# Intermediate columns in batch order, and their loads queued behind the experts' weights, in an attention, MoE and FFN kernel

## The chip, the cores and the metric

The kernel runs on one core of a Trainium2 chip. The metric is device time in microseconds (us) of one execution; the value compared is the median of several runs.

## What is computed

Three stages follow each other; B = 4 batches of S = 576 tokens, 2304 tokens in all, 512 features.

```
x = attention(q, k, v, omega)         # random features, 8 heads, per batch
e = argmax(x @ w_gate)                # an expert for each token
y = gate * (relu(x @ w1[e]) @ w2[e])  # 512 -> 1024 -> 512
h = y @ w_in                          # 512 -> 2048
out = (h * sigmoid(1.702 h)) @ w_out  # 2048 -> 512
```

The inputs are such that the tokens of a batch go to one expert in the main; a loop behind the main part does tokens that go elsewhere.

## The kernel before

All matrix products of the second and third stage are made of three products of halves: an operand is split into a high part (rounded by ACT) and a low part (the rest, by DVE or POOL), and `mm3` (line 110) issues high x high, high x low and low x high into one bank of PSUM.

Attention and experts run interleaved, batch by batch; the code writes the work in an order, and a scheduler then fixes the order of instructions on every engine before the run. An engine takes its instructions strictly in that order, so the first one that has to wait holds up all behind it.

The expert of a batch (`moe_gen`, line 689) takes the 576 tokens in two halves of HS = 288. For each half, layer one makes 8 feature tiles with 4 x 3 matmuls each (tile m_ps), which ACT turns into h1h (relu, line 683) and DVE into h1l (line 686); layer two makes 4 output tiles with 8 x 3 matmuls each, one in a bank of tag m (m_ps) and three in banks of tag a (w_ps), in the last batch or so all four at a time, weights outermost. Half a batch is thus 192 matmuls of 288 columns. DVE takes an output tile out as y (line 736), ACT rounds it to yh (739), POOL, or DVE in the last batch, makes yl (741), and SP stores both to HBM (line 754).

The expert's weights come in eight pieces of 512 KB, c = 0 to 3 of w1 and 4 to 7 of w2 (`stage`, line 611; the DMA is line 623, tile st, two buffers). Each piece is split by ACT into wh (645) and by DVE or POOL into wl (647); a buffer is free for the piece after next once both are done.

y lies in HBM as five chunks of columns, CHUNKS = 512, 512, 512, 512, 256. Columns are ordered in pairs of batches: 512 tokens of the first batch, 512 of the second, then the 64 + 64 tokens that are left of both (`ycol`, line 657). A chunk is loaded by `load_y` (line 882) once all batches that it needs are counted as done: chunks 0 and 1 after batches 0 and 1, chunk 2 after batch 2, chunks 3 and 4 after batch 3. The third stage multiplies each tile f of 128 features of w_in by each chunk c (`first`, tile f_ps, 12 matmuls) in the order f < 3 with c < 3, then c = 3 and 4, then f = 3 and on. `prep_in` (line 851) loads two tiles of w_in (tile raw, line 841, 512 KB each), DVE decodes them (dec), ACT and DVE split them (wi). The result goes through the sigmoid form of gelu to HBM (g_dram) and comes back for blocks of 256 columns (`load_g`), each of which makes two tiles of 128 output rows (`out_rows`).

The transfers of SP stand in one queue. Loads of y, w_in and expert weights are written as jobs that the loop over the last batches calls once a step:

```
        jobs.queue += [load_y(ly, 0), load_y(ly, 1)]
        for n, c in enumerate(Mg):
            tick()
            if wp is None and x_done[0] >= B - 1:
                ...
                jobs.queue += [prep_in(wp, ly, 0), load_y(ly, 2), prep_in(wp, ly, 1)]
            jobs()
```

Of the kernel before, what the change touches and what calls it, by code (L numbers as in the profile page):

```python
# [22 lines left out]
def kernel(  # L23
# [13 lines left out]
    nc = tc.nc  # L37
# [12 lines left out]
    CHUNKS = (4 * P, 4 * P, 4 * P, 4 * P, 2 * P)  # L50
# [57 lines left out]
    wo_dram = dram.tile([7, P, NF2 // 2, DM // 2], F32, name="wo_dram")  # L108

# [547 lines left out]
    def ycol(b, c):  # L657
        base = (b // 2) * 2 * S
        return base + (b % 2) * T * P + c if c < T * P else base + 2 * T * P + (b % 2) * TAIL + c - T * P
# [8 lines left out]
    def moe_gen(b):  # L668
# [3 lines left out]
        for hf in range(2):  # L672
# [46 lines left out]
            for dt in range(KD):  # L719
# [23 lines left out]
                def store(yh=yh, yl=yl, dt=dt, hf=hf):  # L743
                    lo, hi = hf * HS, (hf + 1) * HS
                    for a, z in ((lo, min(hi, T * P)), (max(lo, T * P), hi)):
                        if a < z:
                            o = ycol(b, a)
                            cut = min(z, a + CH - o % CH)
                            for x, e in ((a, cut), (cut, z)):
                                if x == e:  # L750
                                    continue
                                ch, q0 = divmod(o + x - a, CH)
                                for i, t in enumerate((yh, yl)):
                                    nc.sync.dma_start(  # L754
                                        out=y_dram[ch][i][dt * P:(dt + 1) * P, q0:q0 + e - x],
                                        in_=f32(t[:, x - lo:e - lo]),
                                    )
# [3 lines left out]
                if not outer:  # L761
                    yield 1.46
                    pump(1)
        prep["free"] = 2 * NW * (b + 2)

        def count():
            done[0] += 1

        lag(4, count)
# [68 lines left out]
    def load_raw(pool, s, f):  # L838
        raw = pool.tile([P, DM], I64, tag="raw", name="raw", bufs=2)
        if s == 0:  # L840
            nc.sync.dma_start(
                out=raw.rearrange("p (k f) -> p k f", k=KD),
                in_=w_in[:, f * P:(f + 1) * P].rearrange("(k p) f -> p k f", p=P),
            )
        else:
            nc.sync.dma_start(out=raw, in_=w_out[f * P:(f + 1) * P, :])
        return raw
# [3 lines left out]
    def prep_in(pool, rpool, j):  # L851

        raws = [load_raw(rpool, 0, 2 * j + i) for i in range(2)]
# [28 lines left out]
    def load_y(pool, c):  # L882
        while done[0] < (1, 2, 3, 4, 4)[c]:
            yield 1
        y = pool.tile([P, 2, KD, CHUNKS[c]], F32R, tag=f"y{c}", name=f"y{c}", bufs=1)
        for i in range(2):
            nc.sync.dma_start(out=f32(y[:, i]), in_=y_dram[c][i].rearrange("(k p) n -> p k n", p=P))
            if c < 3 and not i:
                yield 3
        y_t[c] = (y[:, 0], y[:, 1])  # L890

    done = [0]
# [10 lines left out]
    if True:  # L903
# [47 lines left out]
        jobs.queue += [load_y(ly, 0), load_y(ly, 1)]  # L951
        for n, c in enumerate(Mg):
            tick()
            if wp is None and x_done[0] >= B - 1:
# [3 lines left out]
                jobs.queue += [prep_in(wp, ly, 0), load_y(ly, 2), prep_in(wp, ly, 1)]  # L958
            jobs()
# [3 lines left out]
        jobs.queue += [load_y(ly, 3), load_y(ly, 4)]  # L963
# [5 lines left out]
        def out_rows(ti):  # L969
            pr, j = divmod(ti, 9)  # L970
            b0 = 2 * pr
            if j < 8:
                b, t = b0 + j // T, j % T
                return [(0, P, out[b * S:b * S + T * P].rearrange("(p t) c -> p t c", t=T)[:, t, :])]
            return [(i * TAIL, TAIL, out[(b0 + i) * S + T * P:(b0 + i + 1) * S, :]) for i in range(2)]
# [42 lines left out]
        def load_g(k, gt, halves=(0, 1)):  # L1018

            c, o = divmod(2 * k * P, CH)  # L1020
            for h in halves:
                nc.sync.dma_start(
                    out=gt[:, h], in_=g_dram[c][h][:, :, o:o + 2 * P].rearrange("f p n -> p f n")
                )
# [276 lines left out]
```

## Time and profile before

| | |
|---|---|
| median of 3 runs | 793.82 us (791.28 to 793.97) |
| profiled execution, its own time | 793.09 us |
| span of the profile (first to last instruction) | 791.3 us |
| mean granted clock of TensorE | 0.987 |
| DMA, mean | 172 GB/s, 136.01 MB |

The stages in the trace: attention with the experts of batches 0 to 2 up to about 320 us, what is left of the experts up to about 411 us, y @ w_in to 605 us, then the product with w_out. In the views below PE is TensorE's matmuls, PEld its weight loads, DVE, ACT, POOL the other engines, SPq the queue of SP. A value in brackets with an arrow is the time an engine stood idle before an instruction and what ended it. The granted clock is a share of 2.4 GHz: 0.50 is 1.2 GHz.

### The profile page before, as it was taken

To read this page: it belongs to the slowest core of one execution; us is meant where nothing else is said; L and a number is where in the kernel's file an instruction comes from. 1 tells how busy PE (TensorE), PEld (TensorE's weight loads), DVE (VectorE), ACT (ScalarE), POOL (GpSimd) and SP (SyncE) were. 2 spreads that over 40 slices of the span, in tenths; PEclk is the share of its full clock that TensorE was granted. 3 is DMA by queue.
4 is the path that set the end of the run, shared out by engine and by line. 5 is a ranking of instruction groups with operands and counts; after the bars stand their busy time and mean duration, and the time that the engine had idled before them with its cause. 6 is when DMAs were issued, how large, how long until landed. Compare 5 with 4: busy or idle time off the path is not lost.

```text
span 791.3 us, 14276 instructions
## 1 busy us (share of the span) xinstructions
PE 762.6 (96%) x5538; PEld 710.2 (90%) x5538; DVE 452.6 (57%) x1026; ACT 305.0 (39%) x575; POOL 177.4 (22%) x134
## 2 busy tenths in 40 slices
PE   7998999999999999979999999999999999999996
PEld 6877899999999999979997888888889999999996
DVE  5877776577764353447320656525044777777761
ACT  5545563345433341423111332244334334434330
POOL 3565297458302450201000223210000000000000
PEclk9999899999999999989999999999999999999998
DMA  5456775368624330698517999993476443444401
GB/s 158 119 141 155 220 205 140 86 155 223 152 53 136 117 93 27 208 296 244 178 30 239 332 385 322 371 386 129 139 229 210 134 134 133 134 134 133 133 28 31
DMA packets 151418, 136.01 MB, mean 172 GB/s; under 512 B 63024, under 2 KB 129840, under 8 KB 150448
## 3 DMA queue, kind: packets, MB, share of 16 engines
q1 hardware_dynamic: 139824, 116.16, 48.3%
q10 hardware_dynamic: 11520, 18.88, 6.5%
q8 instruction: 45, 0.74, 0.4%
q14 instruction: 29, 0.24, 0.1%
HBM read 83.41 MB, written 45.11 MB: 162 GB/s over the span
## 4 chain that ended last, share of the span: by engine, by line
PE 76%; DMA 11%; DVE 4%; SPq 3%; issue 2%; POOL 2%; ACT 2%; POOLq 0%; DVEq 0%; ACTq 0%
PE f_ps L112 22%; PE m_ps L112 15%; PE qa L1049 13%; PE qm L1049 7%; PE pb L1049 3%; DMA st<-in_moe_w_dram 3%; PE w_ps L112 3%; PE num L416 3%; DMA raw<-in_moe_w_in_dram 3%; DMA m<-in_k_dram 2%; PE kv_ps L374 2%; SPq L754 2%; PE pr L316 2%; DMA m<-in_q_dram 2%; PE tq L402 1%
## 5 line engine op out<-in xcount | busy, mean ns | idle before, releaser
L112 PE MATMUL f_ps<-y,wi 128*128 128x512 f32 (+1 forms) x960 | 198.4, 368 | 1.7 <-DMA y<-y_dram 1.7
L112 PEld LDWEIGHTS f_ps<-y,wi 128*128 128x128 f32 x960 | 167.0, 189 | 32.0 <-DMA y<-y_dram 2.1
L1049 PE MATMUL qa<-wo,gs 128*128 128x256 f32 x864 | 107.2, 282 | 0.0
L1049 PEld LDWEIGHTS qa<-wo,gs 128*128 128x128 f32 x864 | 104.8, 190 | 0.0
L995 ACT ACTIVATE g<-f_ps 128x512 f32<-128x512 f32 (+1 forms) x80 | 43.7, 554 | 104.3 <-PE f_ps L112 65.5
L112 PE MATMUL m_ps<-xh,wh 128*128 128x288 f32 x256 | 79.0, 309 | 3.9 <-DVE y L736 3.1
L112 PE MATMUL m_ps<-xh,wl 128*128 128x288 f32 x256 | 76.8, 300 | 0.0
L112 PE MATMUL m_ps<-xl,wh 128*128 128x288 f32 x256 | 76.6, 299 | 0.0
L647 POOL TENSOR_TENSOR wl<-st,wh 128x1024 fp32r<-128x1024 f32 x23 | 54.6, 2382 | 44.9 <-ACT wh L645 41.3
L686 DVE SCALAR_TENSOR_TENSOR h1l<-m_ps,h1h 128x288 fp32r<-128x288 f32 x64 | 28.9, 454 | 62.1 <-ACT h1h L683 62.0
L814 ACT ACTIVATE gs<-s 128x1024 fp32r<-128x1024 f32 x27 | 28.6, 1061 | 75.0 <-DVE s L1034 59.8
L331 DVE TENSOR_REDUCE small<-pr 128x4 f32<-128x512 f32 (+1 forms) x80 | 51.1, 639 | 10.0 <-PE pr L323 5.0
L1049 PE MATMUL qm<-wo,gs 128*128 128x256 f32 x432 | 54.5, 282 | 0.0
L876 POOL TENSOR_TENSOR z<-z 128x256 f32<-128x256 f32 x32 | 25.4, 814 | 127.6 <-DMA g_dram<-g 76.1
L112 PEld LDWEIGHTS m_ps<-xh,wh 128*128 128x128 f32 x256 | 48.7, 190 | 5.3 <-DVE y L736 3.6
L1049 PEld LDWEIGHTS qm<-wo,gs 128*128 128x128 f32 x432 | 52.8, 190 | 0.1
L645 ACT ACTIVATE wh<-st 128x1024 fp32r<-128x1024 f32 (+1 forms) x33 | 34.0, 1032 | 43.5 <-DMA st<-in_moe_w_dram 26.9
L815 DVE TENSOR_TENSOR gs<-gt,gs 128x1024 fp32r<-128x1024 f32 x36 | 44.2, 1226 | 10.4 <-ACT gs L814 9.9
L112 PEld LDWEIGHTS m_ps<-xl,wh 128*128 128x128 f32 x256 | 48.7, 190 | 0.3
L112 PEld LDWEIGHTS m_ps<-xh,wl 128*128 128x128 f32 x256 | 48.8, 191 | 0.0
L112 PE MATMUL m_ps<-h1h,wh 128*128 128x288 f32 x160 | 48.8, 306 | 0.0
L112 PE MATMUL m_ps<-h1h,wl 128*128 128x288 f32 x160 | 47.8, 300 | 0.0
(156 smaller groups left out, 1444.8 us busy)
## 6 DMA issues: line engine op xcount, KB each, us to landing
gt<-g_dram SPq DMA_DIRECT2D x18, 1024.0 KB, 7.2
g_dram<-g ACTq DMA_DIRECT2D x64, 256.0 KB, 5.4
st<-in_moe_w_dram SPq DMA_DIRECT2D x31, 512.0 KB, 4.5
y<-y_dram SPq DMA_DIRECT2D x8, 1024.0 KB, 8.8
raw<-in_moe_w_in_dram SPq DMA_DIRECT2D x16, 512.0 KB, 6.4
raw<-in_moe_w_out_dram SPq DMA_DIRECT2D x16, 512.0 KB, 6.3
wo<-wo_dram SPq DMA_DIRECT2D x7, 1024.0 KB, 7.8
wo_dram<-z SPq DMA_DIRECT2D x8, 768.0 KB, 7.8
```

What stands on the lines that cost most here:

```text
L112: ins = nc.tensor.matmul(out=ps, lhsT=a, rhs=b, start=start and n == 0, stop=stop and n == 2)
L316: nc.tensor.matmul(out=ps[:, :, h2], lhsT=xT[:, (2 * pr + h2) * 2 + t0 // 2], rhs=wbd)
L331: nc.vector.tensor_reduce(out=pm, in_=ps[:, :w], axis=AX.X, op=ALU.max, negate=on_act)
L416: nc.tensor.matmul(out=ps[:n, c, h2, :], lhsT=lhsT, rhs=kv[:, h, :])
L645: nc.scalar.activation(out=hi[:, :, s], in_=st[:, :, s], func=ACTF.Copy)
L647: eng.tensor_tensor(out=lo[:, :, s], in0=st[:, :, s], in1=f32(hi)[:, :, s], op=ALU.subtract)
L686: nc.vector.scalar_tensor_tensor(out=hl[:, f], in0=ps, scalar=0.0, in1=f32(hh[:, f]), op0=ALU.max, op1=ALU.subtract)
L814: nc.scalar.activation(out=hi, in_=src, func=ACTF.Copy)
L815: nc.vector.tensor_tensor(out=lo, in0=src, in1=f32(hi), op=ALU.subtract)
L876: nc.gpsimd.tensor_tensor(out=z[:, o], in0=z[:, a], in1=z[:, b], op=op)
L995: nc.scalar.activation(out=g, in_=ps, func=ACTF.Gelu_apprx_sigmoid)
L1049: ins = nc.tensor.matmul(out=ps, lhsT=x[:, f], rhs=w[i][:, f], start=start and f + m == 0, stop=f == NP - 1 and m == 2, skip_group_check=True,
```

## The change

The columns of y are now in the plain order of batches, in chunks of 512, 512, 512, 480 and 288. `pieces` says in which chunks a run of columns lies. Batches are 576 columns, halves 288: chunks 0 to 3 are 2016 columns, seven halves exactly, and chunk 4 is the last half of batch 3. Work done is counted by halves, and `load_y` waits for the halves that a chunk needs, so chunk 3 does not wait for the last half. The loads of chunks 0 and 1 are no longer asked for as soon as the attention is over: all jobs start when the last expert piece has been staged (`prep["staged"] == 2 * NW * B`), and `behind` ties a load of y, or one of the first four tiles of w_in, to the four entries of SP's queue that were written ahead of it, so that the scheduler puts it after them; no wait is added on the chip. Output rows of a tile are stored in the pieces that the new order gives, two of 64 rows where a tile runs over a boundary, and the eighth block of g is read from chunks 3 and 4 (224 and 32 columns).

```diff
-    CHUNKS = (4 * P, 4 * P, 4 * P, 4 * P, 2 * P)
+    CHUNKS = (4 * P, 4 * P, 4 * P, 480, 288)
...
+    def behind(ins, n):
+
+        eng, me = ins.ins.engine, ins.ins.name
+        found = [i for i in reversed(nc.cur_bb.bb.instructions) if i.engine == eng and i.name != me][:n]
+        for x in found:
+            tc.add_manual_dep(
+                ins.ins, x.name,
+                mybir.DependencyInfo(mybir.DependencyClass.NoSync, mybir.DependencyReason.DATA),
+                reason="behind",
+            )
...
-    def ycol(b, c):
-        base = (b // 2) * 2 * S
-        return base + (b % 2) * T * P + c if c < T * P else base + 2 * T * P + (b % 2) * TAIL + c - T * P
+    done = [0]
+
+    def pieces(c, n):
+
+        found, x = [], 0
+        while x < n:
+            ch = next(i for i in range(NCH) if c + x < sum(CHUNKS[:i + 1]))
+            o = c + x - sum(CHUNKS[:ch])
+            m = min(n - x, CHUNKS[ch] - o)
+            found.append((x, m, ch, o))
+            x += m
+        return found
...
-                    lo, hi = hf * HS, (hf + 1) * HS
-                    for a, z in ((lo, min(hi, T * P)), (max(lo, T * P), hi)):
-                        if a < z:
-                            o = ycol(b, a)
-                            cut = min(z, a + CH - o % CH)
-                            for x, e in ((a, cut), (cut, z)):
-                                if x == e:
-                                    continue
-                                ch, q0 = divmod(o + x - a, CH)
-                                for i, t in enumerate((yh, yl)):
-                                    nc.sync.dma_start(
-                                        out=y_dram[ch][i][dt * P:(dt + 1) * P, q0:q0 + e - x],
-                                        in_=f32(t[:, x - lo:e - lo]),
-                                    )
+                    for x, n, ch, o in pieces(b * S + hf * HS, HS):
+                        for i, t in enumerate((yh, yl)):
+                            nc.sync.dma_start(
+                                out=y_dram[ch][i][dt * P:(dt + 1) * P, o:o + n], in_=f32(t[:, x:x + n])
+                            )
...
+            def count():
+                done[0] += 1
+
+            lag(4, count)
...
-    def load_raw(pool, s, f):
+    def load_raw(pool, s, f, after=0):
         raw = pool.tile([P, DM], I64, tag="raw", name="raw", bufs=2)
         if s == 0:
-            nc.sync.dma_start(
+            ins = nc.sync.dma_start(
                 out=raw.rearrange("p (k f) -> p k f", k=KD),
                 in_=w_in[:, f * P:(f + 1) * P].rearrange("(k p) f -> p k f", p=P),
             )
+            behind(ins, after)
...
-        raws = [load_raw(rpool, 0, 2 * j + i) for i in range(2)]
+        raws = [load_raw(rpool, 0, 2 * j + i, 4 if j < 2 else 0) for i in range(2)]
...
-        while done[0] < (1, 2, 3, 4, 4)[c]:
+        while done[0] * HS < sum(CHUNKS[:c + 1]):
             yield 1
         y = pool.tile([P, 2, KD, CHUNKS[c]], F32R, tag=f"y{c}", name=f"y{c}", bufs=1)
         for i in range(2):
-            nc.sync.dma_start(out=f32(y[:, i]), in_=y_dram[c][i].rearrange("(k p) n -> p k n", p=P))
-            if c < 3 and not i:
+            behind(nc.sync.dma_start(out=f32(y[:, i]), in_=y_dram[c][i].rearrange("(k p) n -> p k n", p=P)), 4)
+            if c + 1 < NCH and not i:
                 yield 3
         y_t[c] = (y[:, 0], y[:, 1])
...
-        jobs.queue += [load_y(ly, 0), load_y(ly, 1)]
         for n, c in enumerate(Mg):
             tick()
             if wp is None and x_done[0] >= B - 1:
                 flush()
                 xep.release()
                 wp = tc.alloc_tile_pool(name="wp", bufs=1)
-                jobs.queue += [prep_in(wp, ly, 0), load_y(ly, 2), prep_in(wp, ly, 1)]
-            jobs()
+                jobs.queue += [prep_in(wp, ly, 0), load_y(ly, 0), load_y(ly, 1), prep_in(wp, ly, 1)]
+                jobs.queue += [load_y(ly, 2), load_y(ly, 3)]
+            if prep["staged"] == 2 * NW * B:
+                jobs()
         flush()
         while jobs.busy():
             jobs()
-        jobs.queue += [load_y(ly, 3), load_y(ly, 4)]
+        jobs.queue.append(load_y(ly, 4))
...
-            pr, j = divmod(ti, 9)
-            b0 = 2 * pr
-            if j < 8:
-                b, t = b0 + j // T, j % T
-                return [(0, P, out[b * S:b * S + T * P].rearrange("(p t) c -> p t c", t=T)[:, t, :])]
-            return [(i * TAIL, TAIL, out[(b0 + i) * S + T * P:(b0 + i + 1) * S, :]) for i in range(2)]
+
+            found, c = [], ti * P
+            while c < (ti + 1) * P:
+                b, k = divmod(c, S)
+                p0 = c - ti * P
+                if k < T * P:
+                    t, p = divmod(k, P)
+                    n = min(P - p, (ti + 1) * P - c)
+                    dst = out[b * S:b * S + T * P].rearrange("(p t) c -> p t c", t=T)[p:p + n, t, :]
+                else:
+                    n = min(S - k, (ti + 1) * P - c)
+                    dst = out[b * S + k:b * S + k + n, :]
+                found.append((p0, n, dst))
+                c += n
+            return found
...
-            c, o = divmod(2 * k * P, CH)
             for h in halves:
-                nc.sync.dma_start(
-                    out=gt[:, h], in_=g_dram[c][h][:, :, o:o + 2 * P].rearrange("f p n -> p f n")
-                )
+                for x, n, c, o in pieces(2 * k * P, 2 * P):
+                    nc.sync.dma_start(
+                        out=gt[:, h, :, x:x + n], in_=g_dram[c][h][:, :, o:o + n].rearrange("f p n -> p f n")
+                    )
```

On SP, where the expert of batch 2 stores its first half and batch 3's weights are being staged (yh, yl are what is stored, st the staged weights, raw w_in), before:

```order
L754 DMA y20_dram_69<-yh_4389 128x288
L887 DMA y0_4015<-y00_dram_65 128x4x512
L887 DMA y0_4015<-y01_dram_66 128x4x512
L887 DMA y1_4205<-y10_dram_67 128x4x512
L887 DMA y1_4205<-y11_dram_68 128x4x512
L754 DMA y21_dram_70<-yl_4390 128x288
L623 ISA
L623 DMA st_4459<-in_moe_w1_dram 128x4x256
```

and now, the rows in the same place, then those around the loads, six stagings later:

```order
L766 DMA y21_dram_70<-yl_4384 128x288
L634 ISA
L634 DMA st_4453<-in_moe_w1_dram 128x4x256
L634 ISA
L634 DMA st_4489<-in_moe_w1_dram 128x4x256
```

and, behind the last staging:

```order
L634 DMA st_4638<-in_moe_w2_dram 128x2x512
L852 DMA raw_4652<-in_moe2_w_in_dram 128x4x128
L852 DMA raw_4654<-in_moe2_w_in_dram 128x4x128
L899 DMA y0_4656<-y00_dram_65 128x4x512
L899 DMA y1_4658<-y10_dram_67 128x4x512
L899 DMA y0_4656<-y01_dram_66 128x4x512
L899 DMA y1_4658<-y11_dram_68 128x4x512
```

The four loads of chunks 0 and 1 went from ahead of piece 2 of the weights to behind piece 7 (st_4638), with the first two tiles of w_in.

On ACT, in the same stage, layer one of batch 2's second half (h1h) and the splits of batch 3's weights (wh1 is piece 1, wh2 piece 2); before:

```order
L645 ACTIVATE wh1_4476<-st_4228 128x1024
L683 ACTIVATE h1h_4392<-m_ps_4461 128x288
L683 ACTIVATE h1h_4392<-m_ps_4480 128x288
L683 ACTIVATE h1h_4392<-m_ps_4497 128x288
L683 ACTIVATE h1h_4392<-m_ps_4516 128x288
L683 ACTIVATE h1h_4392<-m_ps_4533 128x288
L645 ACTIVATE wh2_4512<-st_4459 128x1024
```

and now:

```order
L656 ACTIVATE wh1_4470<-st_4223 128x1024
L703 ACTIVATE h1h_4386<-m_ps_4455 128x288
L703 ACTIVATE h1h_4386<-m_ps_4474 128x288
L656 ACTIVATE wh2_4506<-st_4453 128x1024
L703 ACTIVATE h1h_4386<-m_ps_4491 128x288
L703 ACTIVATE h1h_4386<-m_ps_4510 128x288
L656 ACTIVATE wh3_4542<-st_4489 128x1024
L703 ACTIVATE h1h_4386<-m_ps_4527 128x288
L656 ACTIVATE wh4_4592<-st_4525 128x1024
```

The splits of pieces 2 and 3, which stood behind the last relu of the half, now stand among them: piece 2 ahead of the last three, piece 3 ahead of the last one; piece 4 follows the last. On DVE the low halves of the same pieces moved in the same way, and those of pieces 4, 5 and 6 stand among the evictions y of batch 2 and ahead of the first h1l of batch 3.

On SP, the last stores of batch 3 and the loads behind them; before:

```order
L754 DMA y40_dram_73<-yh_5252 128x128
L754 DMA y41_dram_74<-yl_5253 128x128
L754 DMA y40_dram_73<-yh_5252 128x64
L754 DMA y41_dram_74<-yl_5253 128x64
L887 DMA y3_5287<-y30_dram_71 128x4x512
L887 DMA y3_5287<-y31_dram_72 128x4x512
L887 DMA y4_5290<-y40_dram_73 128x4x256
```

and now:

```order
L766 DMA y40_dram_73<-yh_5247 128x288
L766 DMA y41_dram_74<-yl_5248 128x288
L899 DMA y4_5266<-y40_dram_73 128x4x288
L899 DMA y4_5266<-y41_dram_74 128x4x288
L858 DMA raw_5290<-in_moe2_w_out_dram 128x512
```

The last half is eight stores instead of 24, and chunk 3 is loaded (y3_5071) ahead of them.

## Rows read from the trace of the kernel before

**Rows 1.** The page, part 1: engine, busy us (share of the span), instructions.
```profile
PE 762.6 (96%) x5538; PEld 710.2 (90%) x5538; DVE 452.6 (57%) x1026; ACT 305.0 (39%) x575; POOL 177.4 (22%) x134
```

**Rows 2.** Waits of PE from 320 to 435 us: who, us in total, times, longest.
```profile
PE m_ps L112 <- DVE y L736: 3.1, 2, 2.2
PE w_ps L112 <- ACT wh L645: 2.3, 1, 2.3
PE f_ps L112 <- DMA y<-y_dram: 1.7, 1, 1.7
```

**Rows 3.** Timeline of PE: start us, duration us, instruction, count, [idle before].
```profile
335.59 0.29 PE L112 MATMUL w_ps<-h1l,wh 128*128 128x288 f32 x1
...
345.01 0.30 PE L112 MATMUL m_ps<-xh,wh 128*128 128x288 f32 x1
...
348.90 0.40 PE L112 MATMUL m_ps<-xh,wh 128*128 128x288 f32 x1 [2.15 <-DVE y L736]
...
353.37 0.61 PE L112 MATMUL w_ps<-h1h,wh 128*128 128x288 f32 x1 [2.35 <-ACT wh L645]
...
410.84 19.70 PE L112 MATMUL f_ps<-y,wi 128*128 128x512 f32 x86
...
432.19 172.07 PE L112 MATMUL f_ps<-y,wi 128*128 128x512 f32 x845 [1.66 <-DMA y<-y_dram]
```

**Rows 4.** Chain that ended last, one piece: start us, us, what, count.
```profile
388.91 3.20 PE m_ps L112 x24
```

**Rows 5.** Timeline of PE, a gap in the attention.
```profile
186.93 1.12 PE L402 MATMUL tq<-ident,qp 128*128 128x128 f32 x4 [1.31 <-DVE xl L445]
```

**Rows 6.** Windows: busy us of PE, PEld, DVE, ACT, POOL; granted clock; DMA share; GB/s.
```profile
187.00:190.00 3.00, 3.00 (x20) 2.94 (x21) 2.83 (x8) 1.69 (x4) 3.00 (x2) 0.52 0.68 225
352.00:354.00 2.00, 0.61 (x1) 0.29 (x1) 2.00 (x4) 1.62 (x4) 0.98 (x1) 0.50 0.85 238
432.00:434.00 2.00, 1.80 (x8) 1.51 (x9) 0.00 (x0) 0.60 (x1) 0.00 (x0) 1.00 1.08 389
```

**Rows 7.** Timeline of SP's queue: start us, us, issue, count.
```profile
329.19 2.78 SPq L887 DMA_DIRECT2D y<-y_dram  x4
332.02 0.53 SPq L754 DMA_DIRECT2D y_dram<-yl  x1
332.81 2.30 SPq L623 DMA_DIRECT2D st<-in_moe_w_dram  x1
...
422.06 2.31 SPq L887 DMA_DIRECT2D y<-y_dram  x4
```

**Rows 8.** Tile st, from 300 to 375 us: issue to landing.
```profile
DMA to landing us min/median/max: 3.5/5.1/13.0
```

**Rows 9.** The page, part 6: issues, KB each, median us to landing.
```profile
st<-in_moe_w_dram SPq DMA_DIRECT2D x31, 512.0 KB, 4.5
y<-y_dram SPq DMA_DIRECT2D x8, 1024.0 KB, 8.8
```

**Rows 10.** Timeline of ACT.
```profile
333.26 0.41 ACT L683 ACTIVATE h1h<-m_ps 128x288 fp32r<-128x288 f32 x1 [2.38 <-PE m_ps L112]
...
345.83 1.06 ACT L645 ACTIVATE wh<-st 128x1024 fp32r<-128x1024 f32 x1 [6.85 <-DMA st<-in_moe_w_dram]
```

**Rows 11.** Timeline of DVE.
```profile
346.92 1.23 DVE L647 TENSOR_TENSOR wl<-st,wh 128x1024 fp32r<-128x1024 f32 x1 [7.46 <-ACT wh L645]
...
348.40 0.45 DVE L736 TENSOR_TENSOR y<-m_ps,gb 128x288 f32<-128x288 f32 x1
```

**Rows 12.** Timeline of POOL.
```profile
328.82 1.70 POOL L741 TENSOR_TENSOR yl<-y,yh 128x288 fp32r<-128x288 f32 x1 [7.22 <-DMA y_dram<-yl]
```

**Rows 13.** Timeline, end of the kernel.
```profile
785.19 0.42 DVE L1065 TENSOR_TENSOR ob<-qa,u 128x256 f32<-128x256 f32 x1 [2.45 <-PE qa L1049]
785.65 0.34 SPq L1069 DMA_DIRECT2D out_dram<-ob  x1
```

More of the change, by code (lines that the diff above doesn't have):

```diff
@@ L763, in moe_gen @@
                     pump(1)
+            def count():
+                done[0] += 1
+            lag(4, count)
         prep["free"] = 2 * NW * (b + 2)
-        def count():
-            done[0] += 1
-        lag(4, count)
     def attention_gen():
@@ L886, in load_y @@
         for i in range(2):
-            nc.sync.dma_start(out=f32(y[:, i]), in_=y_dram[c][i].rearrange("(k p) n -> p k n", p=P))
-            if c < 3 and not i:
+            behind(nc.sync.dma_start(out=f32(y[:, i]), in_=y_dram[c][i].rearrange("(k p) n -> p k n", p=P)), 4)
+            if c + 1 < NCH and not i:
                 yield 3
         y_t[c] = (y[:, 0], y[:, 1])
-    done = [0]
     def general_w(pool, f, s):
```

## Prediction, made before the changed kernel ran

> **What bounds the kernel now.** I read the page's first part, then PE's waits between 320 and 435 us, PE's timeline there, the chain that ended last, and last the queues and engines that those waits name.
>
> PE is busy 96% of the span [rows 1]: what can be won is idle time or slow time on PE. Between 320 and 435 us three waits stand out [rows 2]: 3.1 us on m_ps for DVE's eviction y (2.15 of it one wait), 2.3 on w_ps for ACT's wh, 1.7 on f_ps for a load of y. In [rows 3] they are the waits at 348.90, 353.37 and 432.19 us. Behind 432.19 comes a block of 845 matmuls with no wait inside, so whatever is won ahead of it passes to the end.
>
> What do the first two cost? Batch 3's experts stand on PE from 345.01 to 410.84, 65.83 us. The work there is 2 x 192 = 384 matmuls of 288 columns and 24 of f_ps. The chain shows 24 such matmuls in 3.20 us [rows 4], 0.1333 each; [rows 3] show 86 of 512 columns in 19.70, 0.229 each. 384 x 0.1333 + 24 x 0.229 = 56.7. So **9.1 us** are lost: 4.5 in the two waits, the rest in short waits and in matmuls at half clock (0.50 at 352 to 354, [rows 6]). With the 1.66 at 432.19, **10.8 us** lie open.
>
> Their cause is in SP's queue. The four loads of y, 4 MB, are issued at 329.19; behind them the store of a yl, then piece 2 of batch 3's weights at 332.81 [rows 7]. Its landing is the maximum of [rows 8], 13.0 us against a median of 5.1, which gives 345.8; ACT splits it at 345.83 after 6.85 idle [rows 10]; DVE stood 7.46 us before the wl, with the evictions y behind it [rows 11]. That is the 2.15; the 2.35 is the next wh. The 1.66 is chunk 3, which waits for the 24 stores of the last half and is issued at the end of that row, by 422.06 + 2.31 [rows 7].
>
> **The change part by part.**
>
> *Loads of y and of w_in behind the weights.* Removed: all of the 9.1 as it arises now. New is that ACT and DVE have the splits of pieces 2 and 3 ahead of the last relus. I follow two chains.
>
> First, piece 2. The yl ahead of it ends at 330.52 [rows 12], its store takes 0.53 of issue [rows 7], so piece 2 is issued at about 331.3. How long it then takes isn't in the trace of before; bounds are 3.5, the least [rows 8], and 13.0, behind the loads. I take the page's median of all pieces, 4.5 [rows 9], as no load of y is ahead. It lands at 335.8; wh 1.06 [rows 10] to 336.9; relu 0.41 to 337.3, where it ran at 333.26; wl 1.23 [rows 11] to 338.1; the low half to 338.5. PE began layer two at 335.59 [rows 3]. The order now puts its first eleven matmuls or so, those of the ready tiles, ahead of the late one, which PE reaches at 337.06. Wait: **1.4**.
>
> Second, the two buffers. Piece 4 can start once wl of piece 2 is done, 338.2; 4.5 and the two splits take it to 345.0; piece 6 is issued at 345.1, lands at 349.6, wh to 350.7, wl to 351.9. Ahead of the first low half of batch 3 DVE now has that wl, so the low half is there at 352.4. PE comes to it, 24 matmuls (3.2) into batch 3, which starts now at 345.01 + 1.4: 349.7. Wait: 352.4 - 349.7, less one matmul, **2.6**.
>
> A restart costs 0.11 (a first matmul of 0.40 instead of 0.29, [rows 3]); for four, 0.4. The clock: a gap of 1.31 at 186.93 [rows 5] is followed by 0.52 granted in 187 to 190, the gaps before 352 by 0.50, the one of 1.66 before 432.19 by 1.00 [rows 6]. Two gaps of three are followed by half clock, so I count one dip of three us behind the longer wait, 3 x 0.48 = **1.4**; bounds are nothing and two dips, 2.8.
>
> Here the Trainium skill's "TensorE: Matmul & The Clock Gate", section "Why this matters for your kernels", blames throughput drops in the middle of a kernel on gaps without matmuls that are longer than any wait counted here; by it the dip drops out and the sum is 1.4 lower, which is rival B. The row at 187 speaks against it, the one at 432 for it.
>
> *Loads behind everything.* The two tiles of w_in (1 MB), piece 7 (0.5) and the four loads (4 MB) now start at about 348; at 389 GB/s [rows 6] 5.5 MB take 14 us, to 362. PE's first f_ps stands behind 120 matmuls of batch 3, at 346.4 + 2.6 + 1.4 + 120 x 0.1333 = 366.4, so over 4 us are to spare; the stores of batch 2's second half behind them are needed only for chunk 2. Nothing. If the cover is gone, the first f_ps waits by as much as the loads are late.
>
> *The order of columns.* 480 + 288 in place of 512 + 256 are the same 768; linear between 0.1333 at 288 and 0.229 at 512, a pair costs 0.347 against 0.348. Nothing, bounds ±0.3. Chunk 3 no longer waits for the last half: **1.66 gone** (in the 10.8). Chunk 4, issued behind eight stores, has 95 matmuls of 512 and 36 of 480 on PE ahead of it, about 29 us against the 8.8 of a y load [rows 9]. Nothing. The extra pieces of g lie under PE-bound blocks.
>
> *The end.* The last output row tile goes out in two stores of 64 rows; SP's last store is one issue of 0.34 behind DVE [rows 13]: **+0.4**, bounds 0 and 0.7.
>
> Sum: -10.8 + 1.4 + 2.6 + 0.4 + 1.4 + 0.4 = **-4.6**. From the profiled 793.09 that gives 788.5; the median of the runs, 793.82, is 0.7 above. I take the middle of both, 793.45, and forecast **788.9**. Each us of landing costs three: one in the first chain, and in the second, which holds three landings against one that PE has already waited for, two. No gain is left at 4.5 + 4.6 / 3 = 6.0.
>
> **The rivals.**
>
> *A. Pieces land at once and the clock stays up.* With 3.5 instead of 4.5 the waits of 1.4 and 2.6 become 0.4 and 0.6, 3.0 less; the dip (1.4) and a restart (0.1) go too: 788.9 - 4.5 = **784.4**. For it: the least of [rows 8], and HBM then carries little else. Against: the page's 4.5.
>
> *B. As forecast, clock up.* 788.9 - 1.4 = **787.5**. The 1.00 after 1.66 us speaks for it, the 0.52 after 1.31 against.
>
> *C. Waits only move.* At a landing of 5.8, 1.3 over mine, 3.9 us come back: **792.8**, no change that can be told. For it: with two buffers nothing shortens the cycle of load, wh and wl, and the median of 5.1 [rows 8] already costs 1.8.
>
> *D. Slower.* The splits now stand ahead of relus and low halves that PE waits for; before, a late piece of the same half came behind its last relu. With landings like the 8.8 of y's loads [rows 9], 4.3 over mine, 12.9 come back: **801.8**. It decides from 4.5 + 8.9 / 3 = 7.5 for the pieces 2, 4 and 6. Against: no more than the one piece is shown so late, which by itself would cost 8.5, once; the 13.0 arose behind the loads that have gone; what is left beside the pieces is the stores of y and inputs of the attention.
>
> *E. The change does not do what it says.* If the loads still met the weights at HBM, the 9.1 stayed and only the 1.66 went, less 0.4: **792.2**.
>
> The Trainium skill speaks against holding loads back: "DMA: Bandwidth & Descriptors", section "Rules for kernel authors", wants DMAs issued early, work done, and the wait late. By it the loads of y, now at 348 instead of 329, would be the ones waited for. The trace bears it out for y alone, not for the queue: the early loads are what held piece 2 for 13.0 us [rows 8]. Nineteen us later, they would have to take 18 instead of 14 to cost anything, which is part of C.
>
> **How the numbers follow.** Forecast 0.42; A 0.15; B 0.15; C 0.15; D 0.10; E 0.03. A measurement of this kernel tells about 0.5% from no change: 3.97 us, so faster is under 789.85, slower over 797.79. The forecast's own range, by a landing of 4 to 5 (1.5 to either side) and the dip's bounds (1.4), is 786.0 to 791.8; about two thirds of its chance lie under 789.85, so faster is 0.28 + 0.15 + 0.15 = 0.58; slower is D, 0.10; the rest 0.32. The range reaches from just under A, 784.0, over C to 794.0; D is left out, and what A could give beyond its own number.
>
> **What would show it.** In the changed profile: piece 2 landing in 4 to 5.5 us near 336, and ACT idle before its wh; a wait of PE of 1 to 2 us near 337 for a relu or its low half, and one of 2 to 3 near 350 for the first low half of batch 3; granted clock near 0.5 for a few us behind it, if at all; batch 3's last matmul at about 405 (of the 9.1, 5.8 come back: 3.3 less than 410.84, and eleven f_ps fewer ahead: 2.5); no PE wait for y afterwards; two stores of 64 rows last on SP. A landing above 7, a PE wait for y at the first f_ps, or a clock that stays low for long would make it wrong.

## The result and the profile after

The changed kernel takes **787.3 us**, median of 9 runs (784.18 to 789.93), against 793.65 us for the kernel before in as many. The ratio is 0.9908, 95% interval 0.9887 to 0.9930: faster by 0.9%. Forecast were 788.9 us, in a range of 784.0 to 794.0.

The profiled execution took 786.61 us, with a span of 784.8 us and a mean granted clock of 0.991. First the page, part 1, then PE's waits from 320 to 435 us, which answer to [rows 1] and [rows 2]:

```profile
PE 761.8 (97%) x5538; PEld 711.5 (91%) x5538; DVE 453.6 (58%) x1026; ACT 306.4 (39%) x575; POOL 178.8 (23%) x134
```

```profile
PE m_ps L123 <- DVE h1l L706: 1.4, 2, 1.0
PE w_ps L123 <- DVE y L756: 0.2, 1, 0.2
```

Before, the same view had a fourth row that [rows 2] do not show:

```profile
PE m_ps L112 <- DVE h1l L686: 0.6, 1, 0.6
```

Of these 7.7 us of waits 1.6 are left; in none of them was a weight's split or a load of y the last thing that PE waited for. The timeline of PE has them in their places; this answers to [rows 3]:

```profile
345.44 0.29 PE L123 MATMUL m_ps<-xh,wh 128*128 128x288 f32 x1
...
349.00 0.37 PE L123 MATMUL w_ps<-h1h,wh 128*128 128x288 f32 x1 [0.24 <-DVE y L756]
...
350.41 0.40 PE L123 MATMUL m_ps<-xh,wh 128*128 128x288 f32 x1 [1.04 <-DVE h1l L706]
...
355.95 0.40 PE L123 MATMUL m_ps<-xh,wh 128*128 128x288 f32 x1 [0.39 <-DVE h1l L706]
...
401.79 28.49 PE L123 MATMUL f_ps<-y,wi 128*128 128x512 f32 x126
...
597.14 3.03 PE L1070 MATMUL qa<-wo,gs 128*128 128x256 f32 x24
```

and in the trace of before the product with w_out (the expectations below call it the third stage; qa, qm and pb are its banks of PSUM, u a sum on the way, ob a finished tile of the output) began here:

```profile
604.71 3.04 PE L1049 MATMUL qa<-wo,gs 128*128 128x256 f32 x24
```

From batch 3's first matmul to the first of the product with w_out it was 259.70 us before (345.01 to 604.71) and is 251.70 now (345.44 to 597.14): **8.0 us** less. Where they come from stands on SP's queue, which answers to [rows 7], with the landing of st from 300 to 375 us below it, to [rows 8]:

```profile
329.68 0.32 SPq L766 DMA_DIRECT2D y_dram<-yl  x1
330.26 13.09 SPq L634 DMA_DIRECT2D st<-in_moe_w_dram  x5
346.79 0.82 SPq L766 DMA_DIRECT2D y_dram<-yh  x2
348.39 0.32 SPq L766 DMA_DIRECT2D y_dram<-yl  x1
348.95 0.39 SPq L634 DMA_DIRECT2D st<-in_moe_w_dram  x1
349.45 0.96 SPq L852 DMA_DIRECT2D raw<-in_moe_w_in_dram  x2
```

```profile
DMA to landing us min/median/max: 3.4/4.0/4.8
```

Pieces 2 to 6 go out in one row from 330.26 on, and none lands later than 4.8 us after its issue; before, one took 13.0. Piece 2, issued at 330.26, landed after 3.7 us, and ACT begins its split at 334.03 instead of 345.83. On ACT and DVE (these answer to [rows 10, 11]):

```profile
334.03 1.06 ACT L656 ACTIVATE wh<-st 128x1024 fp32r<-128x1024 f32 x1 [2.74 <-DMA st<-in_moe_w_dram]
...
347.37 1.06 ACT L656 ACTIVATE wh<-st 128x1024 fp32r<-128x1024 f32 x1 [0.60 <-DMA st<-in_moe_w_dram]
```

```profile
348.39 0.46 DVE L756 TENSOR_TENSOR y<-w_ps,gb 128x288 f32<-128x288 f32 x1 [0.70 <-POOL yl L761]
348.77 1.22 DVE L658 TENSOR_TENSOR wl<-st,wh 128x1024 fp32r<-128x1024 f32 x1
349.90 0.45 DVE L706 SCALAR_TENSOR_TENSOR h1l<-m_ps,h1h 128x288 fp32r<-128x288 f32 x1
```

The 347.37 is piece 6. Its wl ends on DVE just before the h1l for which PE waits 1.04 us. The clock did not fall behind that wait: three windows of the trace (busy us of PE, PEld, DVE, ACT, POOL; granted clock; DMA share; GB/s), which answer to [rows 6]:

```profile
350.00:352.00 2.00, 1.59 (x12) 1.59 (x13) 1.17 (x3) 0.44 (x1) 0.64 (x1) 1.00 0.91 244
352.00:354.00 2.00, 2.00 (x17) 2.00 (x17) 0.00 (x0) 0.79 (x1) 0.00 (x0) 1.00 1.09 385
354.00:357.00 3.00, 2.61 (x20) 2.38 (x20) 2.70 (x5) 0.98 (x3) 0.00 (x0) 1.00 1.09 372
```

Some of the gain goes back at the end of the kernel. The last ob, which answers to [rows 13]:

```profile
778.30 0.42 DVE L1086 TENSOR_TENSOR ob<-qa,u 128x256 f32<-128x256 f32 x1 [2.45 <-PE qa L1070]
```

From the first matmul of the product with w_out to this row it was 180.48 us before (604.71 to 785.19) and is 181.16 now, 0.7 more; from it to the end of the span 6.11 before (to 791.3) and 6.50 now, 0.4 more.

### The profile page after: what moved, and what is told of

It is laid out like the page before. It is cut to its first block, busy times and chain, and to the rows that moved or that the text cites. A ratio compares the mean times of both kernels' runs of the same rounds, so it can differ in the third digit from the quotient of the medians.

```text
span 784.8 us, 14258 instructions
## 1 busy us (share of the span) xinstructions
PE 761.8 (97%) x5538; PEld 711.5 (91%) x5538; DVE 453.6 (58%) x1026; ACT 306.4 (39%) x575; POOL 178.8 (23%) x134
## 4 chain that ended last, share of the span: by engine, by line
PE 80%; DMA 7%; DVE 5%; issue 4%; POOL 1%; ACT 1%; SPq 1%; POOLq 0%; DVEq 0%; ACTq 0%
PE f_ps L123 24%; PE m_ps L123 18%; PE qa L1070 12%; PE qm L1070 6%; PE w_ps L123 3%; PE pb L1070 3%; PE kv_ps L385 3%; PE num L427 2%; DMA st<-in_moe_w_dram 2%; DMA gt<-g_dram 1%; PE pr L327 1%; DMA m<-in_q_dram 1%; PE tq L413 1%; DMA m<-in_k_dram 1%; PE pr L333 1%
## 5 line engine op out<-in xcount | busy, mean ns | idle before, releaser
L123 PE MATMUL f_ps<-y,wi 128*128 128x512 f32 (+2 forms) x960 | 199.2, 369 | 0.0
L123 PEld LDWEIGHTS f_ps<-y,wi 128*128 128x128 f32 x960 | 169.8, 188 | 28.3
L1016 ACT ACTIVATE g<-f_ps 128x512 f32<-128x512 f32 (+2 forms) x80 | 44.0, 552 | 102.8 <-PE f_ps L123 83.6
L342 DVE TENSOR_REDUCE small<-pr 128x4 f32<-128x512 f32 (+1 forms) x80 | 51.1, 639 | 10.8 <-PE pr L334 6.5
L123 PE MATMUL m_ps<-h1l,wh 128*128 128x288 f32 x160 | 47.7, 299 | 0.0
```

The lines of the kernel that those rows point to most:

```text
L123: ins = nc.tensor.matmul(out=ps, lhsT=a, rhs=b, start=start and n == 0, stop=stop and n == 2)
L342: nc.vector.tensor_reduce(out=pm, in_=ps[:, :w], axis=AX.X, op=ALU.max, negate=on_act)
L1016: nc.scalar.activation(out=g, in_=ps, func=ACTF.Gelu_apprx_sigmoid)
```

## The experiments

Two profiles of one and the same kernel can differ by some 3 us in what lies ahead of batch 3's weights (below: 784.8 and 781.4 us of span for the change). So the traces are compared from a common point: the start of ACT's split of piece 1 of batch 3 to the end of the span. Two repeats say how well this repeats: the change gave 456.9 and 456.6, and runs 6 and 7, which differ in the last store alone, gave 451.02 and 450.96 up to the last ob. The runs' own ratios stand beside it, each to runs of the kernel before made with it (medians 793.1 to 793.9); their intervals are 0.4 to 0.8% wide.

| kernel | split of piece 1 | span | from there to the end | median us | ratio to before (95%) |
|---|---|---|---|---|---|
| before | 327.54 | 791.3 | 463.8 | 793.65 | |
| the change | 327.95 | 784.8 | 456.9 | 787.30 | 0.9908 (0.9887 to 0.9930) |
| 1 loads only | 328.41 | 786.5 | 458.1 | 786.62 | 0.9904 (0.9873 to 0.9935) |
| 2 columns only | 327.79 | 790.2 | 462.4 | 790.51 | 0.9975 (0.9950 to 1.0001) |
| 3 no ties | 325.82 | 785.0 | 459.2 | 788.48 | 0.9949 (0.9925 to 0.9972) |
| 4 y0 early | 326.12 | 788.4 | 462.3 | 790.29 | 0.9971 (0.9950 to 0.9993) |
| 5 the change again | 324.83 | 781.4 | 456.6 | 786.64 | 0.9930 (0.9902 to 0.9957) |
| 6 wl of pieces 6, 7 on POOL | 326.88 | 784.5 | 457.6 | 786.83 | 0.9926 (0.9903 to 0.9950) |
| 7 the same, last store on ACT | 325.50 | 782.5 | 457.0 | 785.61 | 0.9911 (0.9885 to 0.9937) |
| 8 loads only, 6 and 7 on POOL | 327.18 | 783.4 | 456.2 | 786.66 | 0.9913 (0.9888 to 0.9939) |
| 9 y behind piece 2 | 326.76 | 788.4 | 461.6 | 790.71 | 0.9974 (0.9945 to 1.0003) |
| 10 piece 6 on POOL, last store on ACT | 324.52 | 781.7 | 457.2 | 785.36 | 0.9894 (0.9854 to 0.9934) |
| 11 loads only, piece 6 on POOL | 327.10 | 783.1 | 456.0 | 786.00 | 0.9908 (0.9874 to 0.9942) |
| 12 y and w_in behind piece 2 | 328.10 | 785.3 | 457.2 | 787.02 | 0.9938 (0.9913 to 0.9964) |

**1. Only the loads.** The kernel before, with `behind` and the change's place for the loads:

```diff
-        jobs.queue += [load_y(ly, 0), load_y(ly, 1)]
...
-                jobs.queue += [prep_in(wp, ly, 0), load_y(ly, 2), prep_in(wp, ly, 1)]
-            jobs()
+                jobs.queue += [prep_in(wp, ly, 0), load_y(ly, 0), load_y(ly, 1), prep_in(wp, ly, 1)]
+                jobs.queue += [load_y(ly, 2)]
+            if prep["staged"] == 2 * NW * B:
+                jobs()
```

> Only the loads move: y0, y1 and the first w_in tiles go behind the last piece of the weights, as in the change; the columns of y and the chunks stay as before (512, 512, 512, 512, 256). Theory (the queue: the 4 MB ahead of piece 2 are what costs): piece 2 lands in about 4 us, PE's waits between 335 and 360 us sum to under 2 us, the clock stays at 1.00 there, the wait for chunk 3 of about 1.7 us stays; 6 to 7 us faster than before, so about as fast as the change itself, since by the two traces the columns win 1.7 and give back about 0.6 (f_ps of 480 and 288 columns), 0.7 (third stage) and 0.4 (last stores). Rival (the columns: chunk 3 ready earlier and fewer stores are the gain): within 1.5 us of before.

Its waits of PE from 320 to 435 us, and the landing of st:

```profile
PE f_ps L123 <- DMA y<-y_dram: 1.7, 2, 0.9
PE m_ps L123 <- DVE h1l L697: 1.6, 2, 0.9
PE w_ps L123 <- ACT h1h L694: 0.2, 1, 0.2
```

```profile
DMA to landing us min/median/max: 3.6/4.1/4.8
```

As the queue theory had it: no piece is late, the clock is 1.00 in every window from 330 to 360, and the runs are as fast as the change's. The wait for y, expected at 1.7 for chunk 3, is 0.84 for chunk 3 (at 427.62) and 0.89 for chunk 2 (at 386.94). The trace is 1.2 us behind the change. Of that 1.1 lie ahead of batch 3, where PE waited 0.67 for a low half: the store of the yl ahead of piece 2 came 3.0 us after the split of piece 1 instead of 1.7, and piece 2 with it. POOL began that yl late, at 330.50, when the store that frees its buffer had landed; that store took 8.1 us (issued at 322.23), against 7.2 in the change. Why it took longer stays open. The rival falls.

**2. Only the columns.** The change, with the jobs of before and no ties:

```diff
+        jobs.queue += [load_y(ly, 0), load_y(ly, 1)]
...
-                jobs.queue += [prep_in(wp, ly, 0), load_y(ly, 0), load_y(ly, 1), prep_in(wp, ly, 1)]
-                jobs.queue += [load_y(ly, 2), load_y(ly, 3)]
-            if prep["staged"] == 2 * NW * B:
-                jobs()
+                jobs.queue += [prep_in(wp, ly, 0), load_y(ly, 2), prep_in(wp, ly, 1), load_y(ly, 3)]
+            jobs()
```

> Only the columns change: batch order and chunks of 512, 512, 512, 480, 288, out rows and g as in the change; the loads of y0 and y1 stand ahead of piece 2 as before. Theory (the queue): piece 2 still takes about 13 us, the waits of about 2.2 and 2.4 us on PE and the half clock near 352 us stay, the wait for chunk 3 goes; 1.7 - 0.6 - 0.7 - 0.4 = 0.0, so within 1.5 us of before. Rival (the columns): 4 us or more faster than before.

Its waits of PE and the landing of st:

```profile
PE m_ps L123 <- DVE y L756: 2.7, 1, 2.7
PE w_ps L123 <- ACT wh L656: 2.6, 1, 2.6
PE m_ps L123 <- DVE h1l L706: 0.3, 1, 0.3
```

```profile
DMA to landing us min/median/max: 3.6/4.5/13.4
```

The 13 us and both large waits are back; chunk 3's wait is gone. It is 1.4 us less than before by the trace, and the interval just takes in no change. But the 1.4 is not the columns': 1.5 lie in batch 3 (64.37 us, from 345.25 to 409.62, against 65.83), where the granted clock behind the two waits was 0.98 and 0.68 in the two windows of 5 us from 350, against 0.53 and 0.79 before. Behind batch 3 the two traces take the same, 380.6 and 380.5 us. So that 5.7 for the loads (463.8 to 458.1) and this 1.4 come to 7.1, near the change's 6.9, shows nothing about the columns.

**3. No ties.** `behind` is called with 0 for y and w_in; nothing else.

> The change without the ties to four earlier entries of SP's queue; the jobs still start only when the last piece has been asked for. The scheduler now puts the two w_in tiles ahead of piece 2 and the four y loads between pieces 2 and 3. Theory (the queue): piece 2 lands about 3 us later (1 MB ahead of it), piece 3 in 12 to 14 us as it stands behind 4 MB; piece 3's low half and the evictions y behind it are late again, and 4 to 7 us of the gain are lost: 791 to 794. Rival (starting the jobs late is what counts, the ties only tidy up): within 1.5 us of the change, 786 to 789.

```profile
PE w_ps L123 <- ACT h1h L703: 1.6, 1, 1.6
PE m_ps L123 <- DVE h1l L706: 0.7, 1, 0.7
```

```profile
DMA to landing us min/median/max: 3.8/5.3/13.6
```

Neither. Piece 2 came 3.4 us later than in the change, both counted from the split of piece 1 (335.26 less 325.82, against 334.03 less 327.95), and cost these two waits and a clock of 0.81 and 0.85 in the two windows of 5 us from 335. Piece 3 landed after 13.6 us as expected, but PE had no wait at all in batch 3. The loss is 2.3 us by the trace, not 4 to 7; the intervals of the runs overlap with the change's. So a late piece 3 costs nothing, or something covered it; runs 9 and 12 are on that.

**4. A dose: y0 alone ahead of piece 2.** The change with `load_y(ly, 0)` in a runner of its own that starts at once, untied.

> The change with chunk 0's two loads (2 MB) ahead of piece 2 again, all others held back. A dose of the cost in rival D. Theory (piece 2 stands ahead of relus that PE needs, nearly no slack): 2 MB at 389 GB/s make its landing 5.4 us longer, about 9.4; PE waits 4 to 5 us near 337 for a relu or a low half and the clock may dip; 4 to 6 us slower than the change, 791 to 793. Rival (there is slack, the cost before came from 4 MB only): under 1.5 us slower than the change.

```profile
PE w_ps L123 <- ACT h1h L703: 3.5, 3, 2.5
PE m_ps L123 <- DVE h1l L706: 1.6, 2, 0.9
```

```profile
DMA to landing us min/median/max: 3.5/4.5/10.3
```

With half the bytes ahead of it piece 2 lands after 9.7 us (the 10.3 is piece 3), near the 9.4 expected, and the change loses 5.4 us (462.3 to 456.9); the intervals of the runs do not overlap. The cover for piece 2 in the new order is small: this is rival D at the size of one piece.

**5 to 8. The change again, and the wait near 350.** Run 5 is the change itself. In 6 the low halves of pieces 6 and 7 go to POOL; 7 also has the second of the last two stores issued by ACT; 8 is run 1 with the low halves of 6.

```diff
-                eng = nc.vector if (b * 2 * NW + c) in SPLIT_D or b == B - 1 else nc.gpsimd
+                eng = nc.vector if (b * 2 * NW + c) in SPLIT_D or (b == B - 1 and c < 6) else nc.gpsimd
...
-                    nc.sync.dma_start(
+                    (nc.scalar if two and m else nc.sync).dma_start(
```

> The change itself once more, beside the next three. Both theories: 6 to 7 us faster than before. From piece 1's split on ACT to the end 457 us again, piece 2 landing in about 4 us; a wait of PE of about 1 us near 350 and one of 0.4 near 356, both for a low half h1l. Whether piece 2's relu makes PE wait near 337 (0 in the first profile, 0.7 in the run with the loads alone) depends on when its load is issued, so 0 to 0.7 there.

> The change with the low halves of pieces 6 and 7 of batch 3 on POOL instead of DVE; the low halves h1l that stood behind them on DVE are free of them. Theory (the wait near 350 is the one forecast as the second chain: the first low half of batch 3 stands behind wl of piece 6, the one near 356 behind wl of piece 7): both waits go, 1.0 + 0.4 and two restarts of 0.1, 1.5 to 2 us from piece 1's split to the end; the runs may show it as 785 to 786. Rival (PE waits there for ACT's relu or a bank in any case, or DVE and POOL hold each other up): the waits stay or move, under 0.5 us.

> As the run before, and the second of the last two output stores (64 rows each) is issued by ACT, beside SP's. Theory (the tail's 0.4 is the issue of a second store on one queue): the time from the last ob on DVE to the end is 6.1 us as before instead of 6.5. Rival (it is the transfer of two smaller stores): 6.5 stays.

> Only the loads moved, with the columns of before, and the low halves of pieces 6 and 7 on POOL. Theory (columns and loads add up: columns win 2.5 us up to the third stage and give back 1.1 in it and at the end): 1 to 2 us slower than the change with the same low halves on POOL, with 0.8 to 1.7 of wait for chunk 3 left on PE and the third stage 0.7 shorter. Rival (the columns are worth nothing net): within 0.5 us of it.

Run 5 repeats the change: 456.6, waits of 0.97 for the low half and 0.46, piece 2 without a wait. In run 6 the wait near 350 is gone, as theory said; others came in its place, and 0.28 us for a relu at 347.97 beside them:

```profile
PE m_ps L123 <- DVE h1l L706: 1.0, 2, 0.6
PE w_ps L123 <- ACT h1h L703: 0.3, 1, 0.3
```

The two for h1l stand at 356.97 and 360.19, and the second of these rows of DVE tells why:

```profile
353.40 0.46 DVE L706 SCALAR_TENSOR_TENSOR h1l<-m_ps,h1h 128x288 fp32r<-128x288 f32 x1 [2.06 <-ACT h1h L703]
353.77 2.04 DVE L804 TENSOR_SCALAR dec<-raw 128x512 int32<-128x512 int32 x1
```

The decode of w_in, 0.42 us at the median, took 2.04 beside POOL's wl of piece 7 (353.15 to 355.53) and stands ahead of the next low half. No gain: 457.6. Run 7's end is as forecast:

```profile
776.46 0.42 DVE L1086 TENSOR_TENSOR ob<-qa,u 128x256 f32<-128x256 f32 x1 [2.45 <-PE qa L1070]
```

```profile
776.92 0.56 ACTq L1090 DMA_DIRECT2D out_dram<-ob  x1
```

From the ob to the end of the span it is 6.04 us (782.5), against 6.50 and 6.60 with both stores on SP, which speaks for the second issue; run 10, with the same stores as run 7, has 6.25 (775.45 to 781.7), so 0.25 to 0.5 us of it are shown. Run 8, with the columns of before, is 1.4 us ahead of run 6 by the trace and level with it by the runs; no wait for chunk 3 appears. The theory falls; the rival's "within 0.5 us" holds by the runs, while by the trace the new columns cost something.

**9 and 12. What a late piece 3 costs.** In 9 the loads of y0 and y1 are tied to piece 2 alone and stand ahead of piece 3; in 12 the first two tiles of w_in stand there too. Run 9, and what 12 adds:

```diff
-            behind(nc.sync.dma_start(out=f32(y[:, i]), in_=y_dram[c][i].rearrange("(k p) n -> p k n", p=P)), 4)
+            ins = nc.sync.dma_start(out=f32(y[:, i]), in_=y_dram[c][i].rearrange("(k p) n -> p k n", p=P))
+            if c < 2:
+                tc.add_manual_dep(ins.ins, piece2[0], ..., reason="behind")
+            else:
+                behind(ins, 4)
...
+            if f < 2:
+                tc.add_manual_dep(ins.ins, piece2[0], ..., reason="behind")
```

> The change, but y0's and y1's four loads are tied to piece 2 of batch 3's weights only: they stand right behind it and ahead of piece 3; the w_in tiles stay behind piece 7. Theory after the run without ties (its loss of 2.3 us from piece 1's split to the end came from the 1 MB ahead of piece 2; a piece 3 that lands in 13 us holds up nothing that PE needs soon): piece 2 lands in 4 us, piece 3 in 12 to 14, PE has no wait near 337 and no half clock; 0 to 1 us slower than the change from piece 1's split (457 to 458). Rival (4 MB ahead of any piece cost about what they cost before): 4 us or more slower, 461 or more.

> As the run with y0 and y1 right behind piece 2, with the first two w_in tiles there as well (1 MB, then the 4 MB, then piece 3). The scheduler then puts 12 matmuls f_ps into batch 3 where that run had PE wait 3.0 us. Theory (a late piece 3 costs 3 us of wait unless PE has other work at that point; the run without ties lost little because those 12 f_ps stood there): piece 2 lands in 4 us, batch 3 starts 17.5 us after piece 1's split, no wait over 1 us near 350; 455 to 457 from piece 1's split to the end, level with the change or up to 2 us faster. Rival (a late piece 3 costs as much whatever stands on PE): 460 or more.

Run 9 went with the rival, 4.8 us slower than the change. Its waits of PE, then ACT:

```profile
PE w_ps L123 <- ACT h1h L705: 3.0, 1, 3.0
PE f_ps L123 <- DMA y<-y_dram: 1.0, 1, 1.0
PE m_ps L123 <- DVE h1l L708: 0.3, 1, 0.3
```

```profile
346.33 1.06 ACT L658 ACTIVATE wh<-st 128x1024 fp32r<-128x1024 f32 x1 [7.85 <-DMA st<-in_moe_w_dram]
347.29 0.43 ACT L761 ACTIVATE yh<-y 128x288 fp32r<-128x288 f32 x1
347.67 1.06 ACT L658 ACTIVATE wh<-st 128x1024 fp32r<-128x1024 f32 x1
349.82 0.44 ACT L761 ACTIVATE yh<-y 128x288 fp32r<-128x288 f32 x1 [1.09 <-DVE y L758]
350.17 0.69 ACT L705 ACTIVATE h1h<-m_ps 128x288 fp32r<-128x288 f32 x2
```

The relu of batch 3's first tile stands behind the splits of the late piece 3 (landed after 14.4 us) and of piece 4, and behind a yh that waits 1.09 us for DVE's y; that y in turn had the wl of piece 3 ahead of it on DVE and then waited 0.68 us for POOL. Behind the wait the clock was 0.66 over 350 to 355. In run 12 piece 3 is no earlier (landed after 13.6 us, its split at 349.74, later than in run 9 also when counted from piece 1's), but w_in is there, and PE has 12 matmuls f_ps to do at that point. PE's timeline:

```profile
348.74 2.92 PE L123 MATMUL f_ps<-y,wi 128*128 128x512 f32 x12
...
352.21 0.40 PE L123 MATMUL w_ps<-h1h,wh 128*128 128x288 f32 x1 [0.55 <-ACT wh L658]
```

3.0 us of wait become 0.55, the clock stays at 1.00 from 335 to 360, and the trace is level with the change, 457.2 to 456.9. So the order of the loads is not the one cure: what it takes is piece 2 in time, and then either piece 3 in time or other work on PE. That also answers run 3, where the same f_ps stood at 350.77.

**10 and 11. Piece 6 alone on POOL.** Run 10 has `c != 6` in place of `c < 6` in run 7, run 11 in run 8.

> The change with the low half of piece 6 alone on POOL (piece 7's stays on DVE) and the second of the last two stores issued by ACT. Theory (with piece 7 on POOL too, the decode of w_in beside it took 2.04 us on DVE instead of 0.42 and stood ahead of two low halves, which cost the 0.4 and 0.6 near 357 and 360): the wait near 350 goes (1.0 and a restart), the one of 0.4 near 356 stays, those near 357 and 360 are not there, the tail is 6.05: 455.2 from piece 1's split to the end, 1.6 less than the change. Rival (POOL's wl of piece 6 delays yl and with it evictions that PE waits for): 457 again.

> Only the loads moved, columns of before, with piece 6's low half on POOL. Theory (the columns are worth nothing net once the loads have moved: the 1.7 us of waiting for chunk 3 are mostly gone by then, and the third stage and the last stores give back 1.1): 455 to 456 from piece 1's split, level with the run before. Rival (the columns add 1 us or more): 456.5 or more.

Run 10 misses: 457.2, not 455.2. That is the rival's number, by another way: the wait at 350 is gone and so is the slow decode, but PE now waits 0.50 at 351.23 for a relu that stands behind wh of piece 7 on ACT, and 0.80 at 352.56 for the low half behind its wl. Run 11 is at 456.0 as expected. None of 7, 8, 10 and 11 can be told from the change by the runs.

## Why the prediction was right, and where its terms were off

The result, 787.3, lies 1.6 us under the forecast and beside rival B (787.5: as forecast, but the clock stays up). The gain's source was named rightly: the 4 MB ahead of piece 2. Run 1 has the whole gain with the loads alone, run 4 gives 5.4 us of it back with 2 MB. That the number falls beside B's is luck, though, as B keeps the waits of 1.4 and 2.6. By its terms the change is nearer to A (a landing of 3.5, waits of 0.4 and 0.6, no dip), whose sum would be -9.1; what holds it at -6.9 are terms that were put at nothing, the price of the new columns above all. Of the signs that were named, the wait near 337 and the dip did not come, the wait near 350 was half as long or less, and batch 3 ended at 401.79, not at 405; the others came. Term by term:

| term | forecast | measured |
|---|---|---|
| what lay open up to the product with w_out | -10.8 | |
| first chain, piece 2 | +1.4 | 0 |
| second chain, piece 6 and its wl | +2.6 | 1.04 |
| restarts | +0.4 | 0.3 (three) |
| clock | +1.4 | 0 |
| waits not forecast (0.24 and 0.39) | | 0.6 |
| 480 + 288 in place of 512 + 256 | 0 | +1.0 |
| so, from piece 1's split to the product with w_out | -5.0 | -8.0 |
| product with w_out | 0 | +0.7 |
| last stores | +0.4 | +0.4 |
| sum | -4.6 | -6.9 |

- **The first chain** was sized too high. Piece 2 was issued at 330.26, not 331.3, mainly since the yl ahead of it took 0.80 us and not the 1.70 of [rows 12], and landed after 3.7 us, not 4.5, so by 334.03 and not 335.8. In run 1, where it came 1.7 us later (7.76 us after the split of piece 1, against 6.08), the wait is there, 0.67. The place was right, the margin about 1 us.
- **The second chain** was right in place and cause: run 6 takes wl of piece 6 off DVE and the wait near 350 goes. It was 1.04 instead of 2.6, as piece 6 landed by 347.37 and not 349.6; the wl then stood behind an eviction y that waited 0.70 for POOL, which the chain had left out.
- **The clock.** No dip came. The waits were shorter than forecast, and those of 0.97 and 1.04 us (run 5 and the change) left the clock at 1.00; in run 3 the waits of 1.59 and 0.67 were followed by 0.81 over 335 to 340, a mean of the two levels, in run 9 one of 3.03 by 0.66 over 350 to 355. The length of a wait does not settle it: [rows 6] show 1.00 behind 1.66 and 0.52 behind 1.31, and the kernel before and run 2 differ behind much the same waits. What decides stays open. Here the Trainium skill's rule, by which it takes gaps longer than those of the change or of run 3 ("TensorE: Matmul & The Clock Gate", "Why this matters for your kernels"), agrees with the change's trace, but not with run 3's.
- **The columns' price** was costed at nothing, with bounds of 0.3, and is some 1.0 us. Tile by tile in y @ w_in, PE's first matmuls of 512 columns behind the last chunk start 12.40 us apart in the change (498.00 to 547.60 for four tiles) and in run 5, but 12.34 before (493.70 to 555.40 for five) and in run 8, which has the columns of before. The 0.06 on 16 tiles are an estimate of 1.0. (The prediction's linear rule gives 0.349 for either pair, so its 0.347 against 0.348 is a slip; the 0.06 is in neither.) With this term the stretch should have given 7.8 (10.8 less 3.0); 8.0 came.
- **The product with w_out** was costed at nothing and took 0.7 more (0.35 in run 5). PE waits 0.36 there for u, with one more large operation of DVE ahead of it; the rest of the 0.7 stays open.
- **The columns' gain**, 1.66 for chunk 3, was counted in full. The wait does go, but with the loads moved runs 1, 8 and 11 wait 0.84, 0 and 0 for chunk 3 with the old columns, and the new ones give back 1.0 in y @ w_in, 0.35 to 0.7 in the product with w_out and 0.4 at the end. By the traces they cost 1.4 (run 6 against 8) and 1.2 (run 10 against 11); by the runs they are worth nothing that can be told. The gain of the change is the loads'.
- **Costed at nothing, and so:** the loads behind everything. The first f_ps starts at 365.30 without a wait, 1 us before the forecast. (The 14 us for their 5.5 MB are 14.8 in the units of the 389 GB/s, which changes nothing.)
- **Rival D** has its price: one piece 7 us late costs 5.4 (run 4: split 13.17 us after piece 1's, against 6.08). No run shows all pieces late, so its slope of three stays untested.
- **The rule to issue DMAs early** (the Trainium skill, "DMA: Bandwidth & Descriptors", "Rules for kernel authors") was no reason against the change, but run 12 gives it its due: the same loads, 20 us earlier, cost 0.3 us by the trace there, which is no more than the change differs from itself, as long as they stand behind the one transfer that PE needs next.

## What to carry to other kernels

A transfer on a shared queue is priced by what stands behind it: loads that nobody needed yet cost some 6 us here because 512 KB that were needed soon stood behind their 4 MB. Ask which single transfer ends the next wait, put that first, and keep independent matmuls at hand for the point where the next one is late. A wait taken off one engine is only gained if the next instruction in line on PE is ready too: the attempts to take away a wait of 1 us put others in its place, up to ten microseconds later.

## What the runs showed of the hardware

DVE and POOL held each other up when both worked on tiles in SBUF, and whichever began first went through. In the trace of before DVE's wl began at 328.63, and POOL's yl, at 328.82, took 1.70 [rows 12]; in the change POOL was first:

```profile
328.84 0.80 POOL L761 TENSOR_TENSOR yl<-y,yh 128x288 fp32r<-128x288 f32 x1 [6.61 <-DMA y_dram<-yl]
```

```profile
329.05 1.68 DVE L658 TENSOR_TENSOR wl<-st,wh 128x1024 fp32r<-128x1024 f32 x1 [2.09 <-ACT wh L656]
```

1.68 is 1.23 and most of what was left of POOL's 0.80 (0.59 us). The decode of run 6, 2.04 for 0.42, is the same. The Trainium skill says so in "SBUF — State Buffer", section "SBUF: two separate sides": the port pair that the two share is an exclusive lock, not a split of bandwidth. The traces agree but for 0.14 us: the one that was held ended that much before the end of the other plus its own time (330.52 for 330.66, 330.73 for 330.87, 355.81 for 355.95). Here a shift of 0.4 us between the two starts (DVE 0.19 ahead before, POOL 0.21 ahead in the change) let the yl ahead of piece 2 end 1.7 us after the start of piece 1's split (329.64) instead of 3.0 (330.52 in the trace of before): 0.9 of the difference is the hold-up, 0.4 the later start.
